# A two-layer expert network on one core: the second product as seven half-size products, with the partial sums of the first carried between PSUM pairs by ScalarE

## The chip, the cores and the metric

The kernel runs on one core of a Trainium2 chip, as one launch. The metric is device time in microseconds (us); the time before is the median of 3 runs. The profile is of one execution on that core.

## The reference, cut to what matters

Three stages follow each other. Attention with 32 packed queries makes `x` (2304 tokens by 512). A network with 2048 hidden units and `h * cos(h)` makes a new `x` of the same shape. The third stage is a mixture of 8 experts, and the change lies in it:

```
def _moe2_ref(x, w_gate, w1, w2):
    logits = x @ w_gate
    P = np.exp(logits - logits.max())
    for _ in range(8):
        P /= P.sum(1, keepdims=True) + 1e-09
        P /= P.sum(0, keepdims=True) + 1e-09
        P *= N / E
    out = np.zeros((N, D))
    for e in range(E):
        h = np.maximum(x @ w1[e], 0.0)
        ye = h @ w2[e]
        out += P[:, e:e + 1] * ye
    return out
```

N is 2304 tokens, D is 512, E is 8 experts, and each has 1024 hidden units.

## The kernel before, in words

Every large product is made of three matmuls, high part by high part, high by low and low by high, so that float32r operands give nearly float32 results. A value is split by ScalarE (copy to the rounded high part) and by GpSimd or VectorE (value minus high part, the low part).

The third stage loops over 16 units `u` (half an expert, 512 hidden units) and in each over 3 chunks `j` of 768 tokens. A chunk here always means one pair (u, j); there are 48. In a chunk the first product is made the Strassen way (Winograd's form): seven products of half size in each dimension, in the order `MULTS` = 0, 5, 1, 6, 4, 3, 2, in place of eight. One of the seven is called a mult here: 12 matmuls of 128x384 (`g1_mult`, matmuls at L709). The tokens' combinations are made once, kept in HBM as `xd` and loaded again for every unit (`x_load`); the weights' combinations are made by GpSimd (`w1_make`, L667 and L670). Mults go by turns to the PSUM pairs X (banks 2x, 2x+1) and Y of the four banks 0 to 3. Only two of the seven add onto what a pair holds; the other combinations are done by VectorE in SBUF, with the sums `a` to `e` (`add`, L734, one operand from PSUM). Then `relu_split` makes the high and low part of the hidden values (L718 on ScalarE, L719 on VectorE).

The second product of chunk (u, j) is ordinary. `out_g2` and `out_tile` make six tiles of 128 tokens by 512 features, each of 12 matmuls of 128x512 (L780 to L782) in one of the banks 4 to 6; VectorE multiplies the tile with the tokens' probabilities and adds it to `acc` (L793). It is issued one chunk late, between the mults of the next chunk: three tiles after step 2 and three after step 6 (a step is one mult and what is issued around it, numbered n = 0 to 6). Bank 7 serves the logits and the probabilities (`logits`, `sinkhorn`, advanced one piece per step by `step_side`). At the end the last six tiles are made with nothing else beside them, and `acc` goes to `out` as it lies.

All instructions are recorded in program order (the scheduler is manual), so each engine works through its own list in the order in which the code issues it. DMAs are all issued by SP.

Of the kernel before, what the change touches and what calls it, by code (L numbers as in the profile page):

```python
# [8 lines left out]
F32 = mybir.dt.float32  # L9
# [9 lines left out]
P = 128  # L19
# [85 lines left out]
def tile_kernel(ctx: ExitStack, tc: tile.TileContext, qT, kT, v, pT, w_in, w_out, w_gate, w1, w2, out):  # L105
# [105 lines left out]
    raw2 = {}  # L211

    def w2_load(u):
        e, half = divmod(u - U1, 2)
        for i in range(2):
            raw = rawp.tile([P, 2, 512], F32, tag="raw", name="raw32")
            nc.sync.dma_start(out=raw, in_=w2[e, 2 * half + i])
            raw2[u, 2 * i] = raw[:, 0, :]
            raw2[u, 2 * i + 1] = raw[:, 1, :]

    def w2_split(u, f):
        raw = raw2.pop((u, f))
        hi = wp.tile([P, 512], F32R, tag="w2h", name="whi")
        lo = wp.tile([P, 512], F32R, tag="w2l", name="wlo")
        nc.scalar.copy(hi, raw)  # L225
        nc.gpsimd.tensor_tensor(out=lo, in0=raw, in1=hi.bitcast(F32), op=ALU.subtract)  # L226
        w_sb[u, 2, f] = (hi, lo)
# [409 lines left out]
    counts = {"load": 7 * NJ, "use": 0, "bank": 0, "chunk": 0}  # L637
# [15 lines left out]
    def w1_make(u, places):  # L653
        def tile_():
            return pools["w1h"].tile([P, 512], F32, tag="w1h", name="wraw")

        a11, s2, s1, a22, a12, a21 = (tile_() for _ in range(6))
        for i, t in enumerate((a11, a12, a21, a22)):
            nc.sync.dma_start(out=t, in_=w1[u - U1, i])
# [31 lines left out]
    def next_h():  # L691
        slot = slots.pop(0)
        return slot, halves(slot[:, 0:2 * HT]), halves(slot[:, 2 * HT:4 * HT])
# [4 lines left out]
    def g1_mult(u, m, b, start):  # L698

# [4 lines left out]
        for p in range(2):  # L704
            dst = bank[:, 2 * b + p, 0:HT]
# [10 lines left out]
    def relu_split(src, th, q, hb):  # L716
        slot, hi, lo = next_h()
        nc.scalar.activation(hi, src, AF.Relu)  # L718
        nc.vector.scalar_tensor_tensor(  # L719
            out=lo, in0=src, scalar=0.0, in1=hi.bitcast(F32), op0=ALU.max, op1=ALU.subtract  # L720
        )
        hb[q, th] = (hi, lo, slot)

    def g1_steps(u, j):

        hb = h_sb[u, j] = {}
        x = counts["chunk"] % 2
        counts["chunk"] += 1
        y = 1 - x
        X, Y = two_banks(x), two_banks(y)  # L730
        a, b, c, d, e = (halves(t) for t in temps[0:5])

        def add(out, ps, other):
            nc.vector.tensor_tensor(out=out, in0=ps, in1=other, op=ALU.add)  # L734

        g1_mult(u, 0, x, True)
        nc.scalar.copy(a, X)
        yield
        g1_mult(u, 5, y, True)
        add(b, Y, a)  # L740
        yield
        g1_mult(u, 1, x, False)
        relu_split(X, 0, 0, hb)
        yield
        g1_mult(u, 6, y, False)
        add(c, Y, a)
        yield
        g1_mult(u, 4, x, True)
        add(d, X, c)
        relu_split(d, 1, 1, hb)  # L750
        yield
        g1_mult(u, 3, y, True)
        add(e, Y, c)
        relu_split(e, 0, 1, hb)
        yield
        g1_mult(u, 2, x, False)
        add(d, X, b)
        relu_split(d, 1, 0, hb)

    def out_g2(u, j, i):  # L760
        parts = 2 if u == NU - 1 and j == NJ - 1 and i == 2 * TQ - 1 else 1
        for part in range(parts):
            out_tile(u, j, i, part, KD // parts)
        if i % TQ == TQ - 1:
            slots.extend(h_sb[u, j][q, i // TQ][2] for q in range(2))

    def out_tile(u, j, i, part, width):

        t = 2 * TQ * j + i
        e, half = divmod(u - U1, 2)  # L770
        planes = slice(part * width, part * width + width)
        ps = bank[:, 4 + counts["bank"] % 3, 0:P * width]
        counts["bank"] += 1
        th, o = divmod(i, TQ)
        for f in range(4):
# [96 lines left out]
    with tc.manual_schedule():  # L872
# [150 lines left out]
        for s in range(NPLAN, n1):  # L1023
            in_front(s)
            in_back(s)
            if s == n0 + 4:
                w2_load(U1)
# [116 lines left out]
```

## Time and profile before

| | |
|---|---|
| median of 3 runs | 1900.19 us (1899.62 to 1901.01) |
| profiled execution, span from first to last instruction | 1898.9 us |
| median of the runs less that span | 1.3 us |
| TensorE busy | 1877.7 us, 99% |
| VectorE, ScalarE, GpSimd busy | 50%, 31%, 27% |
| third stage, from its first matmul to the end | 386.6 to 1898.9 us |

The profile gives the profiled execution by its span alone; its device time is not listed apart from the runs. Matmul ends are modelled and matmuls overlap, so the pace of TensorE is read from starts and from the chain of work, not from the length of one matmul. In the views PE is TensorE, PEld its weight load, DVE VectorE, ACT ScalarE, POOL GpSimd and SP the engine that issues DMAs.

### The profile page before, as it was taken

The page shows a single profiled execution, that of the slowest core. Times are in us where ns is not written, and L with a number is a line of the kernel's source. Part 1 is how long each engine was busy: PE and PEld are TensorE (multiplying, and loading weights), DVE is VectorE, ACT ScalarE, POOL GpSimd, SP SyncE. Part 2 cuts the span into 40 slices and gives each one's busy share as a digit, 9 for nine tenths or more (in the row PEclk, how much of TensorE's full clock was granted, in tenths as well). Part 3 has the DMA queues.
Part 4 walks back from the last instruction along what each step waited for, and adds up shares of the span by engine and source line. Part 5 has one row for each costly group of instructions (what it writes and reads, how often), then busy time and mean ns, then how long its engine had stood idle before and what let it go on. Part 6 is the DMA issues. An engine that isn't in the chain of part 4 may idle for free.

```text
span 1898.9 us, 27178 instructions
## 1 busy us (share of the span) xinstructions
PE 1877.7 (99%) x11113; PEld 1705.1 (90%) x11113; DVE 948.0 (50%) x1239; ACT 597.6 (31%) x911; POOL 504.0 (27%) x382
## 2 busy tenths in 40 slices
PE   7999999999999999999999999999999999999999
PEld 4799999988999999999999999999999999999998
DVE  5867777575454554443434343444444343434343
ACT  5877777643312122121212121212121212121210
POOL 3445454522122212131303030303030303030300
PEclk9999999999999999999999999999999999999999
DMA  8511111056565656565656565666665565656563
GB/s 287 175 46 45 56 50 52 26 178 210 178 216 177 232 184 224 187 220 192 207 189 205 189 205 196 206 203 205 205 205 206 197 209 186 227 167 227 166 216 117
DMA packets 220524, 335.52 MB, mean 177 GB/s; under 512 B 13936, under 2 KB 199920, under 8 KB 220400
## 3 DMA queue, kind: packets, MB, share of 16 engines
q1 hardware_dynamic: 220400, 333.78, 53.2%
q8 instruction: 88, 1.44, 0.3%
q14 instruction: 36, 0.29, 0.1%
HBM read 312.49 MB, written 21.23 MB: 176 GB/s over the span
## 4 chain that ended last, share of the span: by engine, by line
PE 96%; ACT 1%; DVE 1%; DMA 1%; issue 0%; POOL 0%; SPq 0%; DVEq 0%; ACTq 0%; POOLq 0%
PE bank L709 37%; PE bank L780 14%; PE bank L781 14%; PE bank L782 14%; PE bank L568 11%; PE bank L509 2%; PE bank L511 2%; PE bank L510 2%; PE bank L445 1%; DMA raw<-w_in 0%; DMA k<-kT 0%; PE bank L812 0%; PE bank L302 0%; PE bank L455 0%; PE bank L453 0%
## 5 line engine op out<-in xcount | busy, mean ns | idle before, releaser
L709 PE MATMUL bank<-xh 128*128 128x384 f32 x1344 | 452.6, 337 | 0.0
L709 PE MATMUL bank<-xh,xl 128*128 128x384 f32 x1344 | 450.5, 335 | 0.0
L709 PE MATMUL bank<-xl,xh 128*128 128x384 f32 x1344 | 450.4, 335 | 0.0
L734 DVE TENSOR_TENSOR sum<-bank,sum 128x768 f32<-128x768 f32 x240 | 229.2, 955 | 280.0 <-PE bank L709 277.7
L667 POOL TENSOR_TENSOR xl<-wraw,xh 128x512 fp32r<-128x512 f32 x112 | 161.9, 1451 | 640.0 <-ACT xh L666 626.3
L793 DVE SCALAR_TENSOR_TENSOR acc<-bank,prob,acc 128x512 f32<-128x512 f32 (+1 forms) x253 | 189.0, 747 | 275.6 <-PE bank L782 273.4
L709 PEld LDWEIGHTS bank<-xh 128*128 128x128 f32 x1344 | 252.5, 188 | 7.8 <-ACT acc L787 1.9
L709 PEld LDWEIGHTS bank<-xl,xh 128*128 128x128 f32 x1344 | 252.7, 188 | 3.3
L709 PEld LDWEIGHTS bank<-xh,xl 128*128 128x128 f32 x1344 | 252.6, 188 | 0.0
L781 PE MATMUL bank<-wlo,hreg 128*128 128x512 f32 x580 | 224.8, 388 | 0.0
L780 PE MATMUL bank<-whi,hreg 128*128 128x512 f32 x580 | 224.8, 388 | 0.0
L782 PE MATMUL bank<-whi,hreg 128*128 128x512 f32 x580 | 224.7, 387 | 0.0
L780 PE MATMUL bank<-whi,slot 128*128 128x512 f32 x576 | 224.1, 389 | 0.0
L781 PE MATMUL bank<-wlo,slot 128*128 128x512 f32 x576 | 224.1, 389 | 0.0
L782 PE MATMUL bank<-whi,slot 128*128 128x512 f32 x576 | 224.0, 389 | 0.0
L226 POOL TENSOR_TENSOR wlo<-raw,whi 128x512 fp32r<-128x512 f32 x64 | 83.4, 1313 | 477.3 <-ACT whi L225 477.3
L568 PE MATMUL bank<-hreg,whi 128*128 128x288 f32 x1024 | 187.9, 295 | 0.2 <-DVE rbuf L549 0.2
L718 ACT ACTIVATE hreg<-sum 128x768 fp32r<-128x768 f32 x72 | 61.0, 847 | 332.4 <-DVE sum L734 332.4
L718 ACT ACTIVATE slot<-sum 128x768 fp32r<-128x768 f32 x72 | 61.0, 847 | 327.8 <-DVE sum L734 327.8
L568 PEld LDWEIGHTS bank<-hreg,whi 128*128 128x128 f32 x1024 | 153.1, 188 | 2.0 <-DVE rbuf L549 1.1
L782 PEld LDWEIGHTS bank<-whi,hreg 128*128 128x128 f32 x580 | 108.9, 188 | 22.3
L782 PEld LDWEIGHTS bank<-whi,slot 128*128 128x128 f32 x576 | 108.1, 188 | 22.4
(143 smaller groups left out, 2483.7 us busy)
## 6 DMA issues: line engine op xcount, KB each, us to landing
xh<-xd SPq DMA_DIRECT2D x315, 384.0 KB, 4.1
xl<-xd SPq DMA_DIRECT2D x315, 384.0 KB, 4.8
raw<-w SPq DMA_DIRECT2D x32, 512.0 KB, 6.1
wraw<-w SPq DMA_DIRECT2D x64, 256.0 KB, 5.2
raw<-w_in SPq DMA_DIRECT2D x16, 512.0 KB, 3.8
raw<-w_out SPq DMA_DIRECT2D x16, 512.0 KB, 3.6
xd<-xh SPq DMA_DIRECT2D x21, 384.0 KB, 3.1
xd<-xl SPq DMA_DIRECT2D x21, 384.0 KB, 2.5
```

The source lines that it names most:

```text
L226: nc.gpsimd.tensor_tensor(out=lo, in0=raw, in1=hi.bitcast(F32), op=ALU.subtract)
L509: nc.tensor.matmul(dst, lhsT=mh, rhs=ah, start=(g == 0), stop=False)
L510: nc.tensor.matmul(dst, lhsT=mh, rhs=al, start=False, stop=False)
L568: nc.tensor.matmul(ps[:, di, 0:HC], lhsT=lhsT, rhs=rhs, start=(n in (0, 6)), stop=(n in (17, 23)),)
L667: nc.gpsimd.tensor_tensor(out=lo, in0=src, in1=hi.bitcast(F32), op=ALU.subtract)
L709: nc.tensor.matmul(dst, lhsT=w, rhs=t[:, k, :], start=start and k == 0 and w is a and t is th, stop=k == 1 and w is bq, skip_group_check=True,
L718: nc.scalar.activation(hi, src, AF.Relu)
L734: nc.vector.tensor_tensor(out=out, in0=ps, in1=other, op=ALU.add)
L780: nc.tensor.matmul(ps, lhsT=a, rhs=wh, start=(f == 0), stop=False)
L781: nc.tensor.matmul(ps, lhsT=a, rhs=wl, start=False, stop=False)
L782: nc.tensor.matmul(ps, lhsT=bq, rhs=wh, start=False, stop=(f == 3))
L793: nc.vector.scalar_tensor_tensor(out=dst, in0=ps, scalar=prob[:, t, e:e + 1], in1=dst, op0=ALU.mult, op1=ALU.add)
```

## The change

The second product is made of seven half-size products too. It now makes the output transposed: features on partitions, 384 tokens of a half chunk on the free axis, weights `T` (combinations of w2, made by `t_make` with four subtractions and seven splits per unit on GpSimd) as the stationary operand, combinations of the hidden values as the moving one. A mult of the second product is 12 matmuls of 128x384 (L849), and one is issued after each mult of the first product; the pairs (4, 5) and (6, 7) take them by turns. Its products are numbered 1, 5, 6, 3, 7, 2, 4 in order of use. Since tokens now lie on the free axis, the probabilities can't be a scalar per partition any more: they are written to HBM, loaded broadcast over all partitions (`pb_load`), and multiplied onto the hidden values behind the relu (`relu_scaled`); the first expert's output, made before they are known, is multiplied once (`scale_first`). At the end `out_tile` transposes `acc` back by TensorE, 18 tiles of four transposes, and ScalarE copies them out.

In the first product all but the very first mult of a chunk add onto what their PSUM pair holds. ScalarE copies a partial sum from one pair to the other (Y from X at step 0, X from Y at step 3), so that VectorE keeps two operations there (`b - Y` and `X + b`). The hidden values are kept unsplit in `raw` tiles, VectorE and GpSimd make their combinations, and `h_split` splits them one step ahead of use, in four slots by turns.

```diff
+    def t_make(u):
+        b11, b12, b21, b22 = t_load(u)
...
+        def put(m, src):
+            hi, lo = slots_u[m] = t_place(counts["t"] % 8)
+            counts["t"] += 1
+            nc.scalar.copy(hi, src)
+            nc.gpsimd.tensor_tensor(out=lo, in0=src, in1=hi.bitcast(F32), op=ALU.subtract)
...
+        yield
+        comb(b12, b22, b12)
+        put(7, b12)
...
+    def h_split(s, m, src):
+        slot = slots[counts["h"] % 4]
+        counts["h"] += 1
+        hi, lo = halves(slot[:, 0:2 * HT]), halves(slot[:, 2 * HT:4 * HT])
+        nc.scalar.copy(hi, src)
+        nc.vector.tensor_tensor(out=lo, in0=src, in1=hi.bitcast(F32), op=ALU.subtract)
+        prods[s, m] = (hi, lo)
...
         g1_mult(u, 0, x, True)
...
+        yield
+        nc.scalar.copy(Y, X)
+        yield
+        g1_mult(u, 5, 1 - x, False)
+        yield
+        nc.scalar.copy(b, Y)
         yield
         g1_mult(u, 1, x, False)
...
+        yield
+        relu_scaled(u, j, r22, X, 0)
+        yield
+        g1_mult(u, 6, 1 - x, False)
+        yield
+        nc.scalar.copy(X, Y)
+        nc.vector.tensor_tensor(out=b, in0=b, in1=Y, op=ALU.subtract)
+        yield
+        g1_mult(u, 4, x, False)
+        yield
+        relu_scaled(u, j, r11, X, 1)
+        yield
+        g1_mult(u, 3, 1 - x, False)
+        yield
+        relu_scaled(u, j, r21, Y, 0)
+        nc.vector.tensor_tensor(out=rs, in0=r21, in1=r22, op=ALU.add)
+        nc.gpsimd.tensor_tensor(out=r21, in0=r11, in1=r21, op=ALU.subtract)
         yield
         g1_mult(u, 2, x, False)
...
+        yield
+        nc.vector.tensor_tensor(out=X, in0=X, in1=b, op=ALU.add)
+        relu_scaled(u, j, r12, X, 1)
+        yield
...
+    def g2_mult(u, j, m, banks, tiles, start):
+        th, tl = (halves(t) for t in t_sb[u][m])
+        hh, hl = prods[NJ * u + j, m]
...
+    WIDE = (
+        ((1, 0, BOTH, True, ((1, 1),)),), ((5, 1, BOTH, True, ((2, 2),)),),
+        ((6, 0, BOTH, False, ((1, 2),)),), ((3, 1, BOTH, False, ((1, 2),)),),
+        ((7, 0, BOTH, False, ((2, 2),)),), ((2, 1, BOTH, True, ((1, 1),)),),
+        ((4, 0, BOTH, False, ((2, 1),)),),
+    )
...
                 for n in range(7):
...
+                    step_side()
+                    next(steps)
+                    if prev is not None:
+                        h_steps(s - 1, n + 7)
+                    if n == 6:
+                        h_steps(s, n)
+                    next(steps)
+                    if prev is not None:
+                        g2_step(*prev, n, narrow, pair_no)
...
+                    if s == NJ * NU - 1 and n < 6:
+                        out_tile(0, n, 7)
...
+                    if 7 * j + n in range(1, 8):
+                        next(makes[u], None)
```

In the first two units and the last chunk bank 7 is taken (by the probabilities, by transposes). There a table `NARROW` stands in for `WIDE`: the pair (6, 7) shrinks to bank 6, so that products 5, 3 and 2 run as two halves of 6 matmuls, the second half a step later.

ScalarE, from step 5 of chunk j = 0 of a unit to step 1 of chunk j = 1, in the changed kernel (L741 is the high part in `h_split`, L242 that of a `T` product in `t_make`, L791 the carry from X to Y, L795 the copy of Y to `base`):

```order
L741 CAST hreg<-raw_4001 128x768
L242 CAST thi<-raw_10207 128x512
L741 CAST slot<-raw_4407 128x768
L242 CAST thi<-raw_10209 128x512
L741 CAST hreg<-raw_4410 128x768
L791 COPY bank<-bank 128x2x384
L242 CAST thi<-raw_10209 128x512
L741 CAST hreg<-raw_4410 128x768
L795 COPY base<-bank 128x768
```

Before, the same stretch of ScalarE's list (first the high part of w2, L225, at the end of a unit's first chunk, then one chunk of the first product) was this:

```order
L718 ACTIVATE slot_4416<-sum_4004 128x768
L225 CAST whi<-raw_8678 128x512 x2
L737 COPY sum_4001<-bank 128x768
L718 ACTIVATE hreg<-bank 128x768
L718 ACTIVATE slot_4415<-sum_4004 128x768
L718 ACTIVATE hreg<-sum_4005 128x768
```

The copies that write a PSUM pair now stand behind splits of hidden values and of `T` in one list; before, nothing that TensorE's next mult needed stood there but the relu.

GpSimd, the second half of the making of `T` in the changed kernel (L814 is `r11 - r21` at step 5, L246 a combination of w2, L243 a low part):

```order
L243 TENSOR_TENSOR tlo<-raw_12985,thi 128x512
L243 TENSOR_TENSOR tlo<-raw_12987,thi 128x512
L814 TENSOR_TENSOR raw_4408<-raw_4407,raw_4408 128x768
L246 TENSOR_TENSOR raw_12985<-raw_12987,raw_12985 128x512
L243 TENSOR_TENSOR tlo<-raw_12985,thi 128x512
L243 TENSOR_TENSOR tlo<-raw_12987,thi 128x512
L246 TENSOR_TENSOR raw_12987<-raw_12987,raw_12985 128x512
L243 TENSOR_TENSOR tlo<-raw_12987,thi 128x512
```

The combination for the fifth product (L246 behind L814) waits in the list behind an operation on hidden values; before, GpSimd's list held nothing from hidden values.

VectorE, from the end of step 5 to the end of step 1 of the next chunk, in the changed kernel (L869 adds to `acc`, L742 is the low part in `h_split`, L818 `X + b`, L770 the relu with probabilities, L813, L828 and L831 sums of hidden values):

```order
L813 TENSOR_TENSOR raw_4410<-raw_4408,raw_4000 128x768
L869 TENSOR_TENSOR acc_101<-bank,acc_101 128x2x384
L742 TENSOR_TENSOR hreg<-raw_4407,hreg 128x768
L818 TENSOR_TENSOR bank<-bank,base 128x2x384
L770 SCALAR_TENSOR_TENSOR raw_4409<-bank,pb_3998 128x768
L869 TENSOR_TENSOR acc_101<-bank,acc_101 128x2x384
L742 TENSOR_TENSOR hreg<-raw_4410,hreg 128x768
L828 TENSOR_TENSOR raw_4410<-raw_4410,raw_4407 128x768
L869 TENSOR_TENSOR acc_1628<-bank,acc_1628 128x2x384
L742 TENSOR_TENSOR slot<-raw_4410,slot 128x768
L831 TENSOR_TENSOR raw_4410<-raw_4409,raw_4410 128x768
```

Before, a whole chunk of VectorE's list was this:

```order
L734 TENSOR_TENSOR sum_4002<-bank,sum_4001 128x768
L719 SCALAR_TENSOR_TENSOR slot_4416<-bank,slot_4416 128x768
L793 SCALAR_TENSOR_TENSOR acc_101<-bank,prob,acc_101 128x4x128 x3
L734 TENSOR_TENSOR sum_4003<-bank,sum_4001 128x768
L734 TENSOR_TENSOR sum_4004<-bank,sum_4003 128x768
L719 SCALAR_TENSOR_TENSOR hreg<-sum_4004,hreg 128x768
L734 TENSOR_TENSOR sum_4005<-bank,sum_4003 128x768
L719 SCALAR_TENSOR_TENSOR hreg<-sum_4005,hreg 128x768
L734 TENSOR_TENSOR sum_4004<-bank,sum_4002 128x768
L719 SCALAR_TENSOR_TENSOR hreg<-sum_4004,hreg 128x768
L793 SCALAR_TENSOR_TENSOR acc_101<-bank,prob,acc_101 128x4x128 x3
```

A chunk of VectorE's list grows from 15 operations, of 512 and 768 elements, to 23, all of 768; ten of the 23 read both inputs from SBUF (seven low parts and three sums), where three of the 15 did (L719 from a `sum`).

## Rows read from the trace of the kernel before

**Rows 1.** Page, parts 1 and 2: busy time by engine, granted clock.
```profile
PE 1877.7 (99%) x11113; PEld 1705.1 (90%) x11113; DVE 948.0 (50%) x1239; ACT 597.6 (31%) x911; POOL 504.0 (27%) x382
PEclk9999999999999999999999999999999999999999
```

**Rows 2.** Stretches of the third stage: length, busy PE, PEld, DVE, ACT, POOL, clock, DMA.
```profile
386.60:581.80 195.20, 192.92 (x1035) 171.95 (x1034) 113.01 (x177) 64.32 (x95) 48.10 (x35) 0.99 0.59 196
581.80:1850.20 1268.40, 1268.40 (x6399) 1153.49 (x6398) 541.61 (x633) 249.39 (x350) 267.00 (x197) 1.00 0.61 201
1850.20:1898.90 48.70, 45.44 (x229) 40.09 (x227) 17.58 (x22) 4.16 (x5) 0.00 (x0) 1.00 0.40 119
```

**Rows 3.** Chain of work: start, length, what; four mults in a row.
```profile
1862.66 8.35 PE bank L709 x48
```

**Rows 4.** ScalarE's timeline: the same copy, first and last of 42.
```profile
582.16 0.80 ACT L737 COPY sum<-bank 128x768 f32<-128x768 f32 x1 [6.01 <-PE bank L709]
1850.43 0.80 ACT L737 COPY sum<-bank 128x768 f32<-128x768 f32 x1 [7.04 <-PE bank L709]
```

**Rows 5.** Groups of 581.8 to 1850.2: busy, mean ns, idle before.
```profile
L734 DVE TENSOR_TENSOR sum<-bank,sum 128x768 f32<-128x768 f32 x205 | 195.8, 955 | 244.2 <-PE bank L709 244.2
L719 DVE SCALAR_TENSOR_TENSOR hreg<-sum,hreg 128x768 fp32r<-128x768 f32 x61 | 61.4, 1007 | 58.4 <-ACT hreg L718 58.4
L737 ACT COPY sum<-bank 128x768 f32<-128x768 f32 x41 | 32.9, 802 | 216.6 <-PE bank L709 216.6
L718 ACT ACTIVATE hreg<-sum 128x768 fp32r<-128x768 f32 x61 | 51.7, 847 | 287.1 <-DVE sum L734 287.1
L225 ACT CAST whi<-raw 128x512 fp32r<-128x512 f32 x54 | 33.5, 620 | 40.4 <-PE bank L782 36.7 <-DMA xl<-xd 2.8
L226 POOL TENSOR_TENSOR wlo<-raw,whi 128x512 fp32r<-128x512 f32 x54 | 69.5, 1298 | 429.1 <-ACT whi L225 429.1
L670 POOL TENSOR_TENSOR wraw<-wraw 128x512 f32<-128x512 f32 x52 | 67.4, 1296 | 1.0
```

**Rows 6.** Single lines: count, duration ns min/median/max, first and last start.
```profile
L719 DVE SCALAR_TENSOR_TENSOR hreg<-sum,hreg x53: 957/959/1380, 727.0 to 1781.6; 128x768 fp32r<-128x768 f32 x53
L719 DVE SCALAR_TENSOR_TENSOR hreg<-bank,hreg x18: 958/959/959, 710.9 to 1793.5; 128x768 fp32r<-128x768 f32 x18
L632 DVE TENSOR_TENSOR xl<-sum,xh x7: 943/950/2040, 379.5 to 457.6; 128x768 fp32r<-128x768 f32 x7
L667 POOL TENSOR_TENSOR xl<-wraw,xh x84: 1291/1301/1980, 738.2 to 1782.1; 128x512 fp32r<-128x512 f32 x84
```

**Rows 7.** Timeline: a mult's end on TensorE, and ScalarE behind it.
```profile
1014.80 0.33 PE L709 MATMUL bank<-xh,xl 128*128 128x384 f32 x1
1014.98 0.33 PE L709 MATMUL bank<-xh 128*128 128x384 f32 x1
1015.23 0.80 ACT L737 COPY sum<-bank 128x768 f32<-128x768 f32 x1 [7.04 <-PE bank L709]
```

**Rows 8.** Timeline: VectorE releases TensorE.
```profile
413.48 0.55 DVE L816 COPY l_sb<-bank 128x384 f32<-128x384 f32 x1
414.09 0.31 PEld L819 LDWEIGHTS bank<-ident,l_sb 128*128 128x128 f32 x3 [2.48 <-DVE l_sb L816]
```

**Rows 9.** Timeline: three transposes between two other matmuls.
```profile
434.95 0.49 PE L819 MATMUL bank<-ident,l_sb 128*128 128x128 f32 x3
435.20 0.42 PE L709 MATMUL bank<-xh 128*128 128x384 f32 x1
```

**Rows 10.** Timeline, DMA issues and one group: the end, output and an eviction.
```profile
1870.85 0.39 PE L780 MATMUL bank<-whi,slot 128*128 128x512 f32 x1
1895.68 0.48 DVE L793 SCALAR_TENSOR_TENSOR acc<-bank,prob,acc 128x256 f32<-128x256 f32 x1 [0.95 <-PE bank L782]
out<-acc SPq DMA_DIRECT2D x17, 256.0 KB, 2.6
L787 ACT COPY acc<-bank 128x512 f32<-128x512 f32 x18 | 10.5, 587 | 32.0 <-PE bank L782 32.0
```

More of the change, by code (lines that the diff above doesn't have):

```diff
@@ L724, in g1_steps @@
     def g1_steps(u, j):
-        hb = h_sb[u, j] = {}
+        s = NJ * u + j
         x = counts["chunk"] % 2
         counts["chunk"] += 1
[L729 to L734, printed above, removed]
-        g1_mult(u, 0, x, True)
-        nc.scalar.copy(a, X)
-        yield
-        g1_mult(u, 5, y, True)
-        add(b, Y, a)
+        X, Y = two_banks(x), two_banks(1 - x)
@@ new lines, in g1_steps @@
+        r22, r11, r21, r12, rs = (halves(t) for t in (raws[s % 2], *raws[2:6]))
+        b = halves(base)
+        g1_mult(u, 0, x, True)
+        if u == U1 and j == 0:
+            wh = w_slot(w1_slots[u][0])[0]
+            for p in range(2):
+                nc.tensor.matmul(
+                    bank[:, 2 * (1 - x) + p, 0:HT], lhsT=wh[:, 0, 0:P], rhs=x_slot(0)[0][:, 0, :],
+                    start=True, stop=True, skip_group_check=True,
+                )
+        yield
+        nc.scalar.copy(Y, X)
@@ new lines, in g2_mult @@
+    def g2_mult(u, j, m, banks, tiles, start):
+        th, tl = (halves(t) for t in t_sb[u][m])
+        hh, hl = prods[NJ * u + j, m]
+        for i in tiles:
+            dst = bank[:, banks[i], 0:HT]
+            for p in range(2):
+                a, bq = th[:, p, P * i:P * i + P], tl[:, p, P * i:P * i + P]
+                for w, t in ((a, hh), (a, hl), (bq, hh)):
+                    nc.tensor.matmul(
+                        dst, lhsT=w, rhs=t[:, p, :], start=start and p == 0 and w is a and t is hh,
+                        stop=p == 1 and w is bq, skip_group_check=True,
+                    )
@@ new lines, in g2_step, with pb_load @@
+    def g2_step(u, j, n, narrow, pair_no):
+        sets = ((4, 5), (6, 6)) if narrow else ((4, 5), (6, 7))
+        if pair_no and not narrow:
+            sets = sets[::-1]
+        for m, chain, tiles, start, outs in (NARROW if narrow else WIDE)[n]:
+            g2_mult(u, j, m, sets[chain], tiles, start)
+            for r, d in outs:
+                g2_add(j, r, d, sets[chain], tiles)
+    def pb_load(e, j):
+        row = e * NT + 2 * HT * j
+        nc.sync.dma_start(out=pb[j], in_=p_flat[row:row + 2 * HT].partition_broadcast(P))
@@ new lines, in scale_first, with out_tile @@
+    def scale_first(j):
+        for th in range(2):
+            block = acc_cols(2 * HT * j + HT * th, HT)
+            scale = pb[j][:, HT * th:HT * th + HT].unsqueeze(1).to_broadcast([P, KD, HT])
+            nc.vector.tensor_tensor(out=block, in0=block, in1=scale, op=ALU.mult)
+    def out_tile(j, i, b):
+        t = 2 * TQ * j + i
+        ps = bank[:, b, :]
+        for k in range(KD):
+            nc.tensor.transpose(ps[:, P * k:P * k + P], acc_cols(P * t, P)[:, k, :], ident)
+        rows = rawp.tile([P, DM], F32, tag="raw", name="rows")
+        nc.scalar.copy(rows, ps)
+        nc.sync.dma_start(out=out[P * t:P * t + P], in_=rows)
@@ L815, in logits @@
             )
-        nc.vector.tensor_copy(l_sb, ps[:, 0:HT])
+        nc.scalar.copy(l_sb, ps[:, 0:HT])
         yield
```

291 lines of the change are left out of this document (170 added, 121 removed).

## The prediction

> **What bounds the kernel now.** I read the page first: TensorE is busy 99% of the span at a full granted clock, the other engines half or less [rows 1]. Then the third stage by stretches: from the third unit to the last chunk, 1268.4 us, TensorE has no idle time at all, and it loses some 2 us in the first two units and 3 us in the last chunk and tail [rows 2]. So the third stage costs what its matmuls cost, and a change is worth what it takes from their number and length, less the waits that it brings. The pace is read from the chain of work: four mults in a row, 48 matmuls of 128x384, take 8.35 us, 0.174 us each [rows 3]. The copy that opens each chunk on ScalarE starts at 582.16 and, 41 chunks on, at 1850.43 [rows 4]: 30.93 us per chunk. The 84 matmuls of the first product are 14.61 us of it, which leaves 16.32 us, 0.227 us for each of the 72 matmuls of 128x512.
>
> **TensorE's own gain.** The second product becomes seven mults of 12 matmuls of 128x384: 84 x 0.174 = 14.61 us in place of 16.32. A chunk falls to 29.23 us, 1.71 us less. Over the 41 chunks of the steady stretch that is **-70 us**, over five more in the first two units -8.5 us (the first chunk has no second product beside it). The last chunk's part is counted with the tail below.
>
> **Is the other work hidden in a steady chunk?** A step is now 24 matmuls, 4.18 us: 2.09 for the mult of the first product, 2.09 for that of the second.
>
> VectorE has 23 operations of 768 elements per chunk. The nearest rows take 0.955 to 1.007 us [rows 5], so 23 x 0.955 = 22.0 us of 29.2: it fits with 7 us over. Steps 5 and 6 have four operations (3.8 us), the others three (2.9 us), so none is over its 4.18 us. The ones TensorE waits for have room: the low part is made a step ahead, the add to `acc` empties a pair four half steps before it is written again.
>
> ScalarE has ten operations of 768 elements (0.80 to 0.85 us) and 4.7 of 512 (0.62) per chunk [rows 5]: 11.2 us of 29.2. GpSimd has 22 operations of 512 elements per unit at 1.30 us, and three of 768, for which I take 1.30 x 1.5 = 1.95 us: 11.5 us per chunk.
>
> The tight place is the carry, the copy from one pair to the other, at steps 0 and 3: the next mult of the first product adds onto what it writes, and only one mult of the second product (2.09 us) lies between. ScalarE starts 0.25 us after a mult's last matmul gave way to the next [rows 7], the copy of such a tile takes 0.80 us [rows 5], and TensorE starts 0.06 us after VectorE's end where it waits for it [rows 8]; I take the same after ScalarE. Sum 1.11 us, so 0.98 us is left. A copy that writes PSUM isn't in the trace. Below it is bounded by the eviction of 512 elements, 0.59 us [rows 10], above by twice the row, 1.60 us, which still fits. I take 0.80: same source, same size. In front of it on ScalarE stands a split of hidden values (0.85 us) whose input is ready a step earlier, so I charge nothing; if that cover goes, each late 0.1 us at both carries costs 82 x 0.1 = 8 us.
>
> **One wait that I do expect**, once per unit, at the passage from chunk j = 0 to j = 1. At step 5, counted from its start: the mult ends at 2.09, the relu of `r21` runs from 2.34, the sum `rs` ends at about 4.2, and GpSimd's `r11 - r21`, which overwrites what `rs` reads, runs 4.25 to 6.2. Behind it in GpSimd's list stands the combination for the fifth `T` product, to 7.5, and ScalarE's copy of it (0.62) stands ahead of the first hidden split of step 6 (0.85): that split ends at 9.0. VectorE takes its list in order, so the low part (to 10.0), `X + b` (to 10.9) and the last relu (to 11.9) slip behind it, and the carry of the next step 0 waits for that relu: 11.95 to 12.8, while the mult at step 1 is due at 12.5 (three steps). That is 0.3 us, and about 1 us if GpSimd's low part blocks VectorE's once on the way. I take 0.7 us, bounds 0 and 2: 14 units, **+10 us** (0 to 28). Next late is nothing that TensorE needs: VectorE has made the delay good two steps on.
>
> **Contention.** Where VectorE reads both inputs from SBUF while GpSimd works, its operation grows: the form from `sum` has a median of 959 ns and a longest of 1380, a sum of x 2040, while the form from PSUM never leaves 959; GpSimd's grow from 1301 to 1980 [rows 6]. So the two keep each other out. The mean of the form from `sum` is 1.007 us [rows 5], and GpSimd was at work for a fifth of the time [rows 2]; at two fifths I allow 0.1 us for each of the ten, 1 us per chunk out of the 7 that are free: no charge.
> The Trainium skill states it as a rule (SBUF — State Buffer, Who interferes with whom): an operation of VectorE with two SBUF inputs and a GpSimd operation that reads SBUF lock each other out, for a whole instruction. By that rule alone, with a block each time, the change would end as the first rival below; the trace agrees with the lock, and shows it on a minority of the operations.
>
> **First two units.** In the first chunk nothing covers the carry of step 3: +1.1 us. With `NARROW` only 6 matmuls (1.04 us) lie behind the mult of step 3 in five more chunks: +0.1 each. In the second and third chunk VectorE also makes the sums and low parts of x, eleven operations of 0.95 to 2.04 us [rows 6] (I take 1.1), beside some 16 us of its own and the logits: 28 to 30 us against 29.2, so I charge 2.5 us for each, and 2 us for ScalarE, which does relu, first copies to `acc` and x as well. Together 1.1 + 0.5 + 5 + 2 = 8.6 us of new waits, bounds 2 and 25; with the -8.5 us of shorter matmuls the part comes out at **0**.
>
> **Scaling the first expert's output**: six operations of 1536 elements, about 1.9 us each, in three chunks; one chunk's room holds them, but not the steps they fall on: **+2 us**.
>
> **Last chunk and tail.** Before, from the end of the chunk's first mult: 48.7 us [rows 2]. Now, six mults (12.5), 66 matmuls of the second product (11.5), six transposed tiles. Three transposes took 0.25 us [rows 9], so four 0.35 with the change of operand: 2.1. With narrow waits of 0.4 that is 26.5 us to the last mult of the first product. From there it was 28.05 us (1870.85 to 1898.9) [rows 10]. Now 18 matmuls and seven mults of the second product follow with no first product between them, and VectorE's list sets the pace: 18 operations and a half one at 0.955, 17.7 us, and waits for TensorE and ScalarE at both ends, so the last add ends near 21.7. Three more tiles are transposed (0.35 each), copied (0.59 each) and stored: 2.6 us to land [rows 10], and up to 1.5 more since six tiles leave together. About 28 us again. So 54.5 for 48.7: **+6 us**, bounds 2 and 14.
>
> Loads: each mult's x now has four steps of 4.18 us to land, where mults stood back to back before; `pb` adds 24 loads of 384 KB to a queue that is busy 0.61 [rows 2]. No charge; SP's list holds them behind no wait longer than the step.
>
> **Sum.** 1898.9 - 70 + 10 + 0 + 2 + 6 = 1846.9 us of span; with 1.3 us around it, as before, **1848 us**, a gain of 52 us.
>
> **Rivals.**
> *VectorE becomes the bound* (slower than before). Place: the ten operations per chunk with two SBUF inputs. If each is blocked to the longest row, 2.04 us [rows 6], a chunk is 10 x 2.04 + 13 x 0.955 = 32.8 us against 30.93: 41 x 1.9 = +77 us, 1983 us with the other terms. It decides where the ten average 1.85 us: then 18.5 + 12.4 = 30.9. Against it: they average 1.0 now.
> *The carries stay partly exposed.* ScalarE or VectorE runs half a step late all the time, for reasons as at the passage above, and TensorE waits 0.3 to 0.5 us at both carries: 82 x 0.4 = +33 us, 1881 us. For it: three engines hand each step on in order. Against it: 0.98 us of room at either carry.
> *No wait at all.* GpSimd and VectorE pass each other, and the once-per-unit wait and the first units' waits vanish: 1848 - 10 - 9 = 1829 us.
> *The gain is not there*: the mults of the second product take longer than those of the first, because their operands come fresh from two engines; at 0.194 us per matmul, 16.3 us again, the kernel ends near 1918. Nothing in the rows speaks for it; both are 128x384 with weight loads of the same size.
>
> **How the numbers follow.** My forecast (1838 to 1865) 0.62; carries partly exposed (1865 to 1893) 0.18; no wait at all (below 1838) 0.07; VectorE bound 0.08; no gain in the matmuls or a stop I don't see 0.05. A measurement of this kernel tells about 0.2%, 3.8 us, from no change. Faster: 0.62 + 0.18 + 0.07 = 0.87; the two bad cases share 0.02 for same and 0.11 for slower. The range leaves out the two bad cases and the ends of the others: 1830 to 1882.
>
> **What would show it.** Steady period of 29.2 to 29.6 us per chunk between two copies L791; second-product matmuls 0.174 us apart; at L758 a wait for ScalarE once in three chunks, at step 1 of j = 1, below 1 us. VectorE at 75 to 85% of a steady stretch, ScalarE near 40%. A wait at L758 at step 1 or 4 in every chunk would prove the second rival, VectorE above 95% with TensorE idle the first. I am wrong, too, if the carry copy takes over 1.8 us, or if the tail takes over 40 us behind the last matmul of the first product.

## The result, and the profile after

The changed kernel takes **1871.28 us** (median of 4 runs, 1869.9 to 1873.34) against 1900.6 (4 runs), a ratio of 0.985 (95%: 0.983 to 0.986): 1.5% faster, 23 us above the forecast of 1848 and inside its range. The profiled span is 1868.9 us, where the sum gave 1846.9. Of the 70 us that were to come from TensorE's shorter steady chunks, 60 came. What else is missing lies in the first two units, in the chunks of the scaling and in the tail; the passages cost less than forecast.

The page of the changed kernel, busy time and granted clock, for [rows 1]:

```profile
PE 1825.5 (98%) x11753; PEld 1776.9 (95%) x11753; DVE 1449.8 (78%) x1614; ACT 827.1 (44%) x1248; POOL 774.1 (41%) x542
PEclk9999999999999999999999999999999999999999
```

TensorE is still the bound; VectorE went from 50 to 78%. Now the third stage by stretches, for [rows 2] (columns as there: length, PE, PEld, DVE, ACT, POOL, clock, DMA): the first two units, the three chunks in which the first expert's output is scaled, the steady part, the last chunk and tail.

```profile
386.60:589.17 202.57, 189.26 (x1105) 180.14 (x1105) 160.31 (x217) 104.53 (x156) 84.55 (x56) 0.99 0.57 188
589.17:684.50 95.33, 90.77 (x505) 89.51 (x504) 82.05 (x75) 30.93 (x45) 42.46 (x25) 0.98 0.66 214
684.50:1811.32 1126.82, 1123.22 (x6386) 1119.07 (x6385) 894.96 (x875) 390.17 (x556) 459.38 (x313) 1.00 0.67 216
1811.32:1868.90 57.58, 50.79 (x312) 49.05 (x310) 36.75 (x42) 21.75 (x33) 1.85 (x1) 0.98 0.35 124
```

The steady part holds 38 chunks: 29.65 us each, where it was 30.93 and should have been 29.23 and a share of the passage wait. By these rows TensorE idles 3.6 us in it; but matmul ends are modelled, and the starts show 13 gaps of 0.43 to 0.46 us at the passages, 5.8 us together. That is 0.15 us of the 0.42 that a chunk takes beyond 29.23; nearly all the rest lies inside unbroken runs of matmuls. The copy that opens the third unit and the one that opens the last chunk, 41 chunks apart as in [rows 4]:

```profile
589.17 0.80 ACT L791 COPY bank<-bank 128x768 f32<-128x768 f32 x1
1811.32 0.78 ACT L791 COPY bank<-bank 128x768 f32<-128x768 f32 x1 [5.53 <-PE bank L758]
```

**Where the 22 us lie.** To the first of these rows 7.0 us more than forecast (589.17 for 582.16); between them 1222.15 us for 41 x 29.23 + 10 + 2 = 1210.4, so 11.7 more; in the tail 57.6 for 54.5, 3.1 more. Sum 21.8. Of the 7.0, 1.4 us lie ahead of the first matmul of the first product (387.96 us, before 386.61), 2.8 between it and the same matmul of the third unit, and 2.8 at the first scaling.

**The passage.** The timeline of one passage from j = 0 to j = 1 shows the forecast chain link by link:

```profile
885.50 1.84 POOL L814 TENSOR_TENSOR raw<-raw,raw 128x768 f32<-128x768 f32 x1 [6.50 <-DVE raw L813]
887.31 1.28 POOL L246 TENSOR_TENSOR raw<-raw,raw 128x512 f32<-128x512 f32 x1
888.62 0.62 ACT L242 CAST thi<-raw 128x512 fp32r<-128x512 f32 x1 [10.27 <-POOL raw L246]
889.15 0.83 ACT L741 CAST hreg<-raw 128x768 fp32r<-128x768 f32 x1
889.32 3.27 POOL L243 TENSOR_TENSOR tlo<-raw,thi 128x512 fp32r<-128x512 f32 x2 [0.73 <-ACT thi L242]
890.01 1.42 DVE L742 TENSOR_TENSOR hreg<-raw,hreg 128x768 fp32r<-128x768 f32 x1 [3.48 <-ACT hreg L741]
891.36 0.95 DVE L818 TENSOR_TENSOR bank<-bank,base 128x768 f32<-128x768 f32 x1
892.34 0.96 DVE L770 SCALAR_TENSOR_TENSOR raw<-bank,pb 128x768 f32<-128x768 f32 x1
893.39 0.78 ACT L791 COPY bank<-bank 128x768 f32<-128x768 f32 x1 [2.15 <-DVE raw L770]
894.22 0.44 PE L758 MATMUL bank<-xh 128*128 128x384 f32 x1 [0.28 <-ACT bank L791]
```

`r11 - r21` (L814) holds up the combination for `T` (L246), that ScalarE's copy, that the split, that VectorE's list, that the carry. The low part (L742) runs beside GpSimd's L243 there and takes 1.42 us, in all 13 units 1.41 to 1.42, where it takes 0.96 with GpSimd idle: 0.46 us more, the size of the wait. The matmul at 894.22 starts 0.45 us later than its pace, and so once in each of the 13 units from 716 to 1784; no other gap over 0.3 us is left in that stretch.

**What the forecast did not have.** In the same stretch the start of each matmul, row by row, at the border from the second product (L849) to the first (L758):

```profile
898.35 0.34 PE L849 MATMUL bank<-hreg,tlo 128*128 128x384 f32 x1
898.52 0.34 PE L758 MATMUL bank<-xh 128*128 128x384 f32 x1
898.70 0.33 PE L758 MATMUL bank<-xl,xh 128*128 128x384 f32 x1
898.87 0.34 PE L758 MATMUL bank<-xh,xl 128*128 128x384 f32 x1
899.04 0.34 PE L758 MATMUL bank<-xh 128*128 128x384 f32 x1
899.22 0.35 PE L758 MATMUL bank<-xl,xh 128*128 128x384 f32 x1
899.40 0.34 PE L758 MATMUL bank<-xh,xl 128*128 128x384 f32 x1
899.58 0.34 PE L758 MATMUL bank<-xh 128*128 128x384 f32 x1
899.76 0.33 PE L758 MATMUL bank<-xl,xh 128*128 128x384 f32 x1
```

With the trace's nanoseconds, as the median over 250 borders, the first seven starts are 173, 171, 175, 177, 185, 176 and 182 ns apart, and then exactly 173: a border costs some 26 ns (25 on average over both directions). No wait is shown there; only the starts tell it. The kernel before shows the same pattern behind its two blocks of tiles per chunk, and none at the borders between its own mults, so its pace of 0.174 [rows 3] holds almost none of it. Now a chunk has 14 borders in place of four.

**The scaling and the first unit.** The rows below give the six scalings (single line: count, ns min/median/max, first and last start), the one before the matmul that waits, and what that matmul waits for, an add to `acc` (L869) that stands behind the scaling in VectorE's list; then the logits copy of the first unit, behind the same kind of `T` copy:

```profile
L907 DVE TENSOR_TENSOR acc<-acc,pb x6: 2510/2845/3145, 580.0 to 649.2; 128x1536 f32<-128x1536 f32 x6
583.11 2.85 DVE L907 TENSOR_TENSOR acc<-acc,pb 128x1536 f32<-128x1536 f32 x1
588.71 0.58 PE L849 MATMUL bank<-hreg,thi 128*128 128x384 f32 x2 [2.49 <-DVE acc L869]
421.17 0.62 ACT L242 CAST thi<-raw 128x512 fp32r<-128x512 f32 x1 [4.84 <-POOL raw L246]
421.69 0.47 ACT L932 COPY l_sb<-bank 128x384 f32<-128x384 f32 x1
```

A scaling takes 2.8 us and not 1.9. The gaps in TensorE's starts that go with the scaling are 2.66, 1.87, 0.72, 1.91 and 0.72 us from 588.7 to 656.8, and behind the first some ten matmuls start 0.32 us apart (+1.5 us): 9.4 us, where 2 were charged. The transposes of the logits come 4.53 us late at 422.2.

### The profile page after: what moved, and what is told of

It reads as the page before. It is cut to its first block, busy times and chain, and to the rows that moved or that the text cites. A ratio compares the mean times of both kernels' runs of the same rounds, so it can differ in the third digit from the quotient of the medians.

```text
span 1868.9 us, 29782 instructions
## 1 busy us (share of the span) xinstructions
PE 1825.5 (98%) x11753; PEld 1776.9 (95%) x11753; DVE 1449.8 (78%) x1614; ACT 827.1 (44%) x1248; POOL 774.1 (41%) x542
## 4 chain that ended last, share of the span: by engine, by line
PE 70%; POOL 9%; issue 9%; DVE 7%; ACT 4%; DMA 1%; SPq 0%; POOLq 0%; ACTq 0%; DVEq 0%
PE bank L758 27%; PE bank L849 25%; PE bank L606 11%; POOL tlo L243 4%; POOL raw L246 3%; PE bank L547 2%; DVE hreg L742 2%; PE bank L549 2%; PE bank L548 2%; POOL raw L814 2%; DVE bank L818 1%; DVE raw L770 1%; DVE acc L907 1%; ACT bank L791 1%; PE bank L483 1%
## 5 line engine op out<-in xcount | busy, mean ns | idle before, releaser
L849 PE MATMUL bank<-hreg,thi 128*128 128x384 f32 x2016 | 518.2, 337 | 12.3 <-DVE hreg L742 5.1
L758 PE MATMUL bank<-xh 128*128 128x384 f32 x1344 | 458.9, 341 | 5.1 <-ACT bank L791 5.0
L758 PE MATMUL bank<-xh,xl 128*128 128x384 f32 x1344 | 453.5, 337 | 0.0
L758 PE MATMUL bank<-xl,xh 128*128 128x384 f32 x1344 | 453.4, 337 | 0.0
L869 DVE TENSOR_TENSOR acc<-bank,acc 128x768 f32<-128x768 f32 (+1 forms) x351 | 317.1, 906 | 150.3 <-PE bank L849 146.7
L849 PEld LDWEIGHTS bank<-hreg,thi 128*128 128x128 f32 x2016 | 366.9, 188 | 15.3 <-DVE hreg L742 6.3
L742 DVE TENSOR_TENSOR hreg<-raw,hreg 128x768 fp32r<-128x768 f32 x252 | 313.8, 1245 | 49.7 <-ACT hreg L741 48.2
L849 PE MATMUL bank<-hreg,tlo 128*128 128x384 f32 x1008 | 340.4, 338 | 0.0
L741 ACT CAST hreg<-raw 128x768 fp32r<-128x768 f32 x252 | 209.7, 836 | 139.4 <-DVE raw L770 44.9
L758 PEld LDWEIGHTS bank<-xh 128*128 128x128 f32 x1344 | 252.7, 188 | 14.8 <-ACT bank L791 10.1
L758 PEld LDWEIGHTS bank<-xl,xh 128*128 128x128 f32 x1344 | 253.4, 189 | 0.0
L758 PEld LDWEIGHTS bank<-xh,xl 128*128 128x128 f32 x1344 | 253.2, 188 | 0.0
L243 POOL TENSOR_TENSOR tlo<-raw,thi 128x512 fp32r<-128x512 f32 x112 | 157.7, 1419 | 208.2 <-ACT thi L242 208.2
L814 POOL TENSOR_TENSOR raw<-raw,raw 128x768 f32<-128x768 f32 x48 | 89.4, 1862 | 315.7 <-DVE raw L813 315.7
L849 PEld LDWEIGHTS bank<-hreg,tlo 128*128 128x128 f32 x1008 | 189.4, 188 | 0.0
L849 PE MATMUL bank<-slot,thi 128*128 128x384 f32 x672 | 172.2, 337 | 0.1
L770 DVE SCALAR_TENSOR_TENSOR raw<-bank,pb 128x768 f32<-128x768 f32 x168 | 160.0, 952 | 13.4 <-PE bank L758 12.0
L242 ACT CAST thi<-raw 128x512 fp32r<-128x512 f32 x112 | 69.6, 621 | 191.5 <-POOL raw L246 191.5
```

The source lines that it names most:

```text
L242: nc.scalar.copy(hi, src)
L243: nc.gpsimd.tensor_tensor(out=lo, in0=src, in1=hi.bitcast(F32), op=ALU.subtract)
L741: nc.scalar.copy(hi, src)
L742: nc.vector.tensor_tensor(out=lo, in0=src, in1=hi.bitcast(F32), op=ALU.subtract)
L758: nc.tensor.matmul(dst, lhsT=w, rhs=t[:, k, :], start=start and k == 0 and w is a and t is th, stop=k == 1 and w is bq, skip_group_check=True,
L770: nc.vector.scalar_tensor_tensor(out=out, in0=src, scalar=0.0, in1=scale, op0=ALU.max, op1=ALU.mult)
```

## The experiments

Theory: what the kernel loses beside its bare pace is (1) the border cost, (2) the passage's chain, here and in the first unit, (3) the long scalings in VectorE's list. Rival: GpSimd, VectorE and TensorE slow each other as a whole, so that no single edit gives much back. The changed kernel itself ran beside the first three as an anchor. The later runs are compared with it too, since the kernel before took 1900.6 to 1900.9 us beside each set of them.

> The changed kernel itself, as the anchor for the three runs beside it. All theories: 1871 us (0.985 of the kernel before), 88.96 us between the carries L791 of one j in two successive units, and one wait of 0.60 to 0.63 us at L758 in each unit from the fourth on.

Measured 1870.58 us, 0.984 of before (0.983 to 0.985).

**The combination a step earlier**

```diff
         put(3, b22)
-        yield
         comb(b12, b22, b12)
+        yield
         put(7, b12)
```

> Only the place of one GpSimd subtraction in its list changes: the combination for the fifth T product is issued a step earlier, ahead of r11 - r21 instead of behind it. Theory of the prediction (the wait at L758 once per unit comes down the chain GpSimd, ScalarE's copy of T, the split, VectorE, the last relu, the carry): the 13 gaps of 0.6 us at j = 1 go, 13 x 0.44 = 5.7 us, and the 4.7 us gap of the first unit, whose logits copy stands behind the same copy of T, shrinks by some 4 us: 1860 to 1863 us in all, a unit of 88.5 us. Rival (VectorE or GpSimd is slowed by the other at that place, and the order of GpSimd's list has no part in it): the gaps stay, 1870 to 1872 us.

Measured 1860.2 us, 0.978 (0.977 to 0.980), 10.4 below the anchor. The waits at L758 are gone from every unit from the fourth on; the windows row of the stretch has TensorE without a pause, and a chunk takes 29.47 us:

```profile
684.50:1800.00 1115.50, 1115.50 (x6361) 1115.50 (x6360) 896.26 (x871) 389.75 (x553) 471.18 (x313) 1.00 0.67 217
```

At a passage the low part and the carry are now these:

```profile
883.05 1.72 DVE L742 TENSOR_TENSOR hreg<-raw,hreg 128x768 fp32r<-128x768 f32 x1
888.48 0.78 ACT L791 COPY bank<-bank 128x768 f32<-128x768 f32 x1 [5.51 <-PE bank L758]
```

So the order of GpSimd's list decides: VectorE's low part is lengthened still more, to 1.72 us, but it starts early enough that the carry waits for TensorE alone. In the changed kernel the late start and the 0.46 us of lengthening together made the wait. Against the anchor's trace the third stage is 9.8 us shorter, 6.8 of it from the fourth unit to the last chunk and 2.9 in the first two units, where the 4.53 us became 1.75 and, a little later, 1.73.

**The scaling in pieces**

```diff
+                    if i in (1, 2) and n < 4:
+                        scale_first(i, (n,))
```

> The scaling of the first expert's output in the second and third of its three chunks is cut into pieces of 768 elements, one each at steps 0 to 3, in place of two pieces of 1536 at step 5. Theory (the waits of 2.83, 2.04, 2.08 and 0.9 us between 585 and 657 us are VectorE's list, held up by operations of 2.5 to 3.1 us): the two later chunks lose some 4 us of waits, 1867 us, and the steady chunks are the same to 0.01 us. Rival (the waits there come from the first loads of the probabilities or from x's): no change, 1871 us.

Measured 1865.19 us, 0.981 (0.979 to 0.982), 5.4 below the anchor (four runs, 1860.97 to 1866.58); the four waits of 0.7 to 1.9 us became one of 0.43, which is that unit's passage: 4.8 us less. The edit also moves these scalings, and the load of probabilities behind each, to earlier steps; the waits that went had ended with VectorE's L742 and ScalarE's L791, none with a DMA. The two edits together:

> The two edits that gained by themselves, together: the combination of w2 a step earlier (1860.2 us alone, -10.4) and the scaling in pieces of 768 (1865.2 alone, -5.4). If they remove different waits, as their rows say: -15.8, 1855 us (1853 to 1857). If VectorE's list is what both relieve, they overlap: 1858 to 1860 us.

Measured 1854.32 us, 0.976 (0.974 to 0.977): 16.3 below the anchor; the two gains add up to 15.8.

**The carries late by one copy**: each carry (`nc.scalar.copy(Y, X)` and `nc.scalar.copy(X, Y)`) stands twice in ScalarE's list.

> The changed kernel, with both carries issued twice on ScalarE, so that each is 0.8 us later. The prediction's theory (0.98 us of room at either carry, except where the chain of the passage makes it late): the steady chunks keep their 29.65 us but for the passages, whose wait of 0.44 grows by 0.8 to 1.2 us, 14 x 0.8 = +11 us, 1882 us (1880 to 1886). Rival (the carries are all but exposed in every chunk): 82 x 0.8 = +66 us, 1937 us; half of that if only one of the two is tight.

Measured 1887.57 us, 0.993 (0.992 to 0.994), 17 above the anchor. The passage's gap grew from 0.45 to 1.26 us in each unit, 0.8 as forecast, and chunks without a passage keep 29.47 us, so both carries do have 0.8 us of room there. The rest, some 6 us, came in the first two units and the scaled chunks.

**The carries on VectorE**

```diff
-        nc.scalar.copy(Y, X)
+        nc.vector.tensor_copy(Y, X)
...
-        nc.scalar.copy(X, Y)
+        nc.vector.tensor_copy(X, Y)
```

> The changed kernel with the two carries of a chunk copied by VectorE instead of ScalarE: the part of the change that gives them to ScalarE is undone. VectorE then has 25 operations of 0.96 us in a chunk of 29.65, 81%. Prediction's theory (at either carry there is about 1 us of room): a carry on VectorE stands in its list behind the low part alone, and takes 0.96 in place of 0.78, so the steady chunks hold and only passages and first units lose: 1871 to 1878 us. Rival (VectorE's list is already so late that whatever is added to it at steps 0 and 3 shows): 82 x 0.3 = +25 us or more, 1895 us.

Measured 1988.08 us, 1.046 (1.045 to 1.048), 117 us above the anchor: both expectations missed. Its timeline at a passage, and the windows row behind it:

```profile
938.75 0.96 DVE L770 SCALAR_TENSOR_TENSOR raw<-bank,pb 128x768 f32<-128x768 f32 x1
939.62 0.95 DVE L869 TENSOR_TENSOR acc<-bank,acc 128x768 f32<-128x768 f32 x1
940.49 0.95 DVE L742 TENSOR_TENSOR hreg<-raw,hreg 128x768 fp32r<-128x768 f32 x1
941.47 1.90 DVE L828 TENSOR_TENSOR raw<-raw,raw 128x768 f32<-128x768 f32 x1
943.29 0.95 DVE L791 COPY bank<-bank 128x768 f32<-128x768 f32 x1
944.30 0.69 PE L758 MATMUL bank<-xh 128*128 128x384 f32 x1 [3.95 <-DVE bank L791]
944.40:949.90 5.50, 5.50 (x18) 5.50 (x19) 2.53 (x3) 1.35 (x2) 0.00 (x0) 0.52 0.08 7
```

ScalarE's carry waits for the last relu (L770) only; VectorE's stands behind three more operations of its list, 3.7 us. Elsewhere in the steady chunks no gap was over 0.33 us; each passage lost 4.1 us. And TensorE, idle for 4 us, came back at a granted clock of 0.52, near the lower level (1.2 GHz), with some 16 matmuls 0.32 us apart: 2.7 us more. A unit takes 95.5 us for 88.96. Of the 119 us between this trace and the anchor's, 85 lie from the fourth unit to the last chunk, 12 in the third unit and 23 in the first two. VectorE at 76% of the span was not full; the order of its list decided.

**Fewer borders, three ways.** First the second product's mults in three early groups:

```diff
-                        g2_step(*prev, n, narrow, pair_no)
+                        for k in (n,) if narrow else {0: (0, 1), 3: (2, 3, 4), 5: (5, 6)}.get(n, ()):
+                            g2_step(*prev, k, narrow, pair_no)
```

> The same matmuls, but in all chunks with the wide table the seven mults of the second product are issued in three groups (two behind step 0, three behind step 3, two behind step 5), so TensorE goes to and fro between the two products six times a chunk instead of 14. Theory (each change from one product to the other costs TensorE about 26 ns, whatever else runs): 8 x 0.026 = 0.21 us per chunk over 41 chunks, -8.5 us, and the carries at steps 0 and 3 get two or three mults of cover in place of one, so that the 0.6 us waits of the passages go as well, -5.7 us: 1857 us, and a steady unit of 87.9 us. Rival (the slower starts come from operands and banks that other engines have just written, not from the change itself): the lost time stays per mult, only the passages can gain, 1865 us or more; and if the groups make VectorE's adds to acc late, TensorE waits at the fourth and seventh product and the time goes above 1871 us.

Measured 1909.02 us, 1.004 (1.003 to 1.005): 38 us above the anchor. A split is made one step ahead of use, so the second and third mult of a group come before theirs. TensorE's timeline inside a group:

```profile
904.73 0.33 PE L849 MATMUL bank<-hreg,thi 128*128 128x384 f32 x1
905.83 0.44 PE L849 MATMUL bank<-hreg,thi 128*128 128x384 f32 x1 [0.77 <-DVE hreg L742]
```

Gaps of 0.9 to 1.3 us of this kind sum to 41 us in the stretch from 716 to 1780 us. The starts, though, bear on the border: groups of 24 and 36 matmuls, as those of 12 before, show the same seven irregular starts once, at their head, and none inside. The cost is one for a change of product, not for a mult, a bank pair or a new operand tile.

Then late groups, on the kernel with the two gaining edits: the same table as `{0: (0,), 3: (1, 2, 3), 6: (4, 5, 6)}`.

> Upon the two edits of the run beside it: the mults of the second product in groups again, but each group is issued late instead of early (one behind step 0, three behind step 3, three behind step 6), so that every split is made two half steps or more before its use, which the early groups lacked. TensorE goes to and fro six times a chunk instead of 14. Theory (27 ns per change from one product to the other, by whatever cause; the loss of the early groups was the late split alone): 8 x 0.027 x 39 = -8 us, 1847 us (1844 to 1850), a unit of 87.9 us. Rival (three mults of the first product in a row take away the time in which ScalarE and VectorE carry sums and empty banks): waits at steps 3 to 6 in every chunk, 0.3 us or more each, 1865 us and above.

Measured 1885.82 us, 0.992 (0.991 to 0.994), 31 above the kernel that it stands on. Now ScalarE is late, with three steps' work in 6.3 us; its timeline, and TensorE behind it:

```profile
931.36 0.62 ACT L710 CAST xh<-wraw 128x512 fp32r<-128x512 f32 x1
931.88 0.84 ACT L741 CAST hreg<-raw 128x768 fp32r<-128x768 f32 x1
932.62 0.62 ACT L710 CAST xh<-wraw 128x512 fp32r<-128x512 f32 x1
933.13 0.83 ACT L741 CAST hreg<-raw 128x768 fp32r<-128x768 f32 x1
934.07 0.59 PE L849 MATMUL bank<-hreg,thi 128*128 128x384 f32 x2 [1.14 <-ACT hreg L741]
```

Weight splits (L710), in another chunk those of `T`, stand ahead of the hidden split: 1.3 us in two chunks of three. The third chunk has no wait and takes 29.28 us for 29.47, 0.19 for eight borders: 24 ns each.

Last, milder groups, `{0: (0,), 2: (1, 2), 3: (3,), 6: (4, 5, 6)}` (eight borders) and `{0: (0,), 1: (1,), 2: (2,), 3: (3,), 6: (4, 5, 6)}` (ten):

> The two gaining edits, with the second product's mults in groups at steps 0 (one), 2 (two), 3 (one) and 6 (three): eight changes of product in a chunk instead of 14, and no group later than two steps. Theory (a change costs 25 ns on average; the late groups lost 31 us only because three mults of the first product in a row leave 6.3 us for the ScalarE work of three steps): 6 x 0.025 x 41 = -6 us, 1848 us. Rival (two steps' ScalarE work in 4.2 us is too much as well): waits at step 2 or 3 in two of three chunks, 0.5 us each or more, 1865 us.

> As the run beside it, but only the last three mults of a chunk's second product in one group, at step 6: ten changes of product instead of 14. Theory: 4 x 0.025 x 41 = -4 us, 1850 us, with no wait in the steady chunks, since the late groups' run had none at step 6. Rival (the change of product costs nothing that grouping can give back): 1854 us or more.

Measured 1852.69 us, 0.975 (0.974 to 0.976), and 1854.43 us, 0.976 (0.974 to 0.977). A unit takes 88.1 and 88.2 us for 88.4, some 4.5 and 2.7 us over the kernel; both gave 2.6 to 2.8 us back in the scaled chunks, where grouped mults waited for VectorE. As times they can't be told from 1854.32: what they gain shows in the trace alone.

**The border and the banks.** The first product's pairs become banks (0, 1) and (4, 5), the second's (2, 3) and (6, 7):

```diff
-        return bank[:, 2 * b:2 * b + 2, 0:HT]
+        return bank[:, far["pair"] * b:far["pair"] * b + 2, 0:HT]
...
-        sets = ((4, 5), (6, 6)) if narrow else ((4, 5), (6, 7))
+        sets = ((2, 3), (6, 6)) if narrow else ((2, 3), (6, 7))
```

> Upon the same two edits: only the places in PSUM change. The pairs of the first product are banks (0, 1) and (4, 5), those of the second (2, 3) and (6, 7), so that of the 14 borders in a chunk seven lie between banks of one half (0 to 3, or 4 to 7) and seven between the halves; before all 14 were between the halves. Theory A (the 27 ns are the cost of moving from one half of the banks to the other): seven borders lose nothing, 7 x 0.027 x 41 = -7.7 us, 1847 us. Theory B (they are the cost of moving to other operands, from w1 and x to T and hidden values and back): no change, 1855 us, and the pattern of starts at all 14 borders.

Measured 1854.93 us, 0.976 (0.975 to 0.977), a chunk of 29.47 us, and the pattern at all 14 borders: theory A is refuted. That the operands make the cost is what is left of the two, but it was not shown by itself.

**The best version**: two edits more.

```diff
+                        scaled = s - NJ * (U1 + 1) - 2 in (1, 2)
-                        for k in (n,) if narrow else {0: (0,), 2: (1, 2), 3: (3,), 6: (4, 5, 6)}.get(n, ()):
+                        for k in (n,) if narrow or scaled else {0: (0,), 2: (1, 2), 3: (3,), 6: (4, 5, 6)}.get(n, ()):
...
-                    if i == 0 and n == 5:
-                        scale_first(0)
-                        pb_load(1, 0)
+                    if i == 0 and n >= 5:
+                        scale_first(0, (0, 1) if n == 5 else (2, 3))
+                        if n == 6:
+                            pb_load(1, 0)
```

> The two gaining edits and the groups at steps 0, 2, 3 and 6, with two more: in the two chunks where the scaling of the first expert's output runs at steps 0 to 3, the mults go one per step (there the groups made waits of 1.58 and 1.05 us), and the scaling of the first chunk is spread over steps 5 and 6 (its four pieces in a row took 6.06 us of VectorE and made a wait of 2.8 us, behind which eleven matmuls started 0.32 us apart). Theory (these waits are VectorE's list alone): -2.6 and up to -4.3 from 1852.7, 1846 to 1850 us. Rival (the later load of the probabilities, or x's, then makes the next chunk wait): the first gain alone, 1850 us, or worse.

Measured **1847.26 us**, 0.972 (0.971 to 0.973): 23.3 below the anchor, 5.4 below the groups alone. Its windows of the scaled chunks and of the steady part:

```profile
584.36:672.40 88.04, 88.04 (x504) 88.04 (x503) 82.43 (x81) 31.31 (x45) 39.70 (x25) 1.00 0.71 227
672.40:1787.90 1115.50, 1115.50 (x6385) 1114.01 (x6385) 860.23 (x875) 390.13 (x555) 480.82 (x313) 1.00 0.67 217
```

TensorE has no idle time left in these rows, from the third unit to the last chunk. The wait behind the first scaling, just ahead of them, fell from 2.80 to 1.06 us, although the load of the probabilities behind it comes a step later, so the rival does not hold there.

## Why the prediction was right, and where it was off

The measured 1871 us lies inside the stated range, but not in the band of the forecast's own mechanism (1838 to 1865); it lies in the band of the second rival (1865 to 1893), whose mechanism did not occur. What brought it there are terms that were mis-sized or not in the sum at all. So the direction and the main term were understood; that the range held the sum of the errors was in part luck.

*TensorE's own gain, -70 us*: the mechanism was right, the size off by some 10 us. The pace is 0.1733 us and 168 matmuls give 29.12, but 14 borders add 0.35: the chunk without waits takes 29.47 and not 29.23, and the 41 chunks gained 60 us. The step that was mis-sized: the pace was taken from mults in a row [rows 3] for a program in which no two mults of one product follow each other.

*The passage, +10 us*: right in place and chain, shown by the earlier combination. It cost 0.45 us per unit in place of 0.7, 6 us in all. The forecast had 0.3 us for the chain alone and more if VectorE was blocked on the way; with one operation lengthened by 0.46 the sum was 0.45, so the chain alone would about have reached the mult. The wait for the logits in the first unit has in part the same root and was not seen.

*Scaling, +2 us*: mis-sized, 9.4 us. The operation reads two SBUF operands of 1536 elements beside a busy GpSimd and takes 2.5 to 3.1 us; the pieces, one per step, showed that the long stretch in VectorE's list made the waits.

*First two units, 0*: 2.8 us, as 196.0 us for 193.2 between the first matmuls of the first product in the first and the third unit. The gaps over 0.9 us in it (4.53, 1.98, 1.79, 1.15, 1.03, 0.91) sum to 11.4 where 8.6 were charged in all, and the longest, the logits' wait on ScalarE's list, was not among the charges. *Tail, +6*: +8.9, from 48.7 to 57.6. The last matmul of the first product starts 26.45 us in, as forecast; behind it came 31.1 us where 28 were taken, with the last add to `acc` ending at 23.7 and not 21.7. No run tried the tail.

*Hidden work in the steady chunk*: right. VectorE is busy 894.96 / 38 = 23.6 us of a chunk (22.0 and 1 were allowed). The allowance for contention was small: in the groups of the steady stretch (busy, mean ns, idle before) the low part with two SBUF inputs stands beside the add from PSUM:

```profile
L742 DVE TENSOR_TENSOR hreg<-raw,hreg 128x768 fp32r<-128x768 f32 x200 | 251.6, 1258 | 36.2 <-ACT hreg L741 34.9
L869 DVE TENSOR_TENSOR acc<-bank,acc 128x768 f32<-128x768 f32 x266 | 254.0, 955 | 129.1 <-PE bank L849 127.7
```

0.3 us more on average, 0.1 expected, and nothing on the PSUM form. By their times, 150 of the 266 low parts of the stretch ran beside a GpSimd operation, and 125 of these took more than 1.01 us, up to 1.96; of the 116 others none took over 0.96. As many of the adds from PSUM ran beside GpSimd, and none of them took over 0.96. No delay was over 1.0 us. The trace agrees with the Trainium skill's rule of the lock (SBUF — State Buffer, Who interferes with whom) in which operations are held up and beside what, and shows it at most of the places where the two met. The prediction's "minority" was true of the kernel before, where 13 of the 39 that met grew; the median of 959 ns hides the change.

VectorE as the bound stayed far off all the same: the ten operations with two SBUF inputs averaged 1.20 us, where 1.85 would decide. (That rival's 1983 us leaves out the passage's 10 us.) ScalarE is at 35% of the steady part, not near 40, and the period of 29.65 us lies just above the 29.2 to 29.6 that were to show the forecast.

*The carries*: 0.78 us for the copy that writes PSUM, 0.80 taken. That both have 0.8 us of room off the passage was shown by issuing them twice, so the second rival (1881 us), near in time, is not what happened. The third (no wait at all) is refuted by the passage, and the fourth by the pace. What stays open: what in the change of product costs the 26 ns, and the remaining waits of the first two units; two of these end in the trace with ScalarE's first copies to `acc`, which no run tried to move.

## What to carry to other kernels

When a shorter product is interleaved with another, measure TensorE's pace where the two alternate, not in a run of one. When a copy is given to an engine with time to spare, count what stands ahead of it in that engine's list: the same carry cost nothing on ScalarE off the passage, and moving it to VectorE, 76% busy, cost 117 us, part of it through TensorE's clock. Operations on one engine that wait for another one's late work belong behind, not ahead of, what third engines wait for: one subtraction moved by one step gave 10 us.

## What the hardware showed that was not expected

Each change from one product to the other cost 24 to 28 ns on TensorE, spread over the first seven matmuls, with no wait in the trace, the same in groups of 12, 24 and 36 matmuls and the same with other PSUM banks. After an idle time of 4 us the granted clock was 0.52 over 5.5 us, and matmuls of 128x384 started 0.32 us apart in place of 0.173. One copy of 128x768 from PSUM to PSUM took ScalarE 0.78 us and VectorE 0.95. A VectorE operation on 128x768 float32 values with both inputs in SBUF took 0.96 us with GpSimd idle and up to 1.96 beside it; with one input in PSUM it stayed at 0.96 or less either way.
